# A second exchange through DRAM, read back by five transfers on one queue instead of four on two

## The chip, the cores and the metric

The kernel runs on one core of a Trainium2 chip. The metric is the device time of one execution in microseconds (us); lower is better. The kernel before takes 1402.76 us, the median of three runs (1402.32, 1402.76 and 1404.93).

The core's engines appear in the profile as PE (TensorE, the matrix engine, with PEld for its weight loads), DVE (VectorE), ACT (ScalarE), POOL (GpSimd) and SP (SyncE, which here only issues transfers). Each engine works off its own list of instructions in order and waits on semaphores for the others. A transfer is issued by an instruction on an engine's list and lands later; the profile lists the issuing instructions as SPq and ACTq.

## What is computed

Two layers of the same pair: a spectral filter over a 2048 x 512 activation, then multi-query attention with 32 heads of 16 columns that share one key and one value head.

```python
def _A_ref(x, w_r, w_i):
    X = rfft2(x.astype(float32))            # 2048 x 512 -> 2048 x 257
    X = X * (w_r + 1j * w_i)
    return irfft2(X, s=(S, D)).astype(bfloat16)

def _B_ref(x, wq, wk, wv, wo):
    q = (x @ wq) in 32 heads of 16; k = x @ wk; v = x @ wv
    p = softmax(q k^T * 16 ** -0.5)
    return (p v, heads joined) @ wo

x = x + _A_ref(layernorm(x)); x = x + _B_ref(layernorm(x))
x = x + _A_ref(layernorm(x)); x = x + _B_ref(layernorm(x))
```

## The kernel before

**The spectral layer.** `spectral_layer` does the 2-D transform as matrix products. A transform of length 2048 is split into 128 x 16, and between its two steps the data have to change their place across the 128 partitions. That is done by an exchange: tiles are written from the on-chip memory to a DRAM buffer and read back in another order. There are two exchanges in a layer, one on the way forward (D1) and one on the way back (D2). The columns stand in two halves, h = 0 and h = 1, and each half is exchanged by itself.

**The second exchange.** `back(j)` (lines 361 to 376) finishes a step of the inverse transform: PE computes, ACT (for the last piece DVE, line 373) copies the result into B1, and SP issues a write of 128 KB from B1 to D2 (line 376). Eight such writes make one half. `cross2` (lines 378 to 380) reads D2 back into B2. B2 holds 16 tiles t of 128 x 256 for each half; four reads of 256 KB bring tiles 0 to 3, 4 to 7, 8 to 11 and 12 to 15. All eight writes of a half must have landed before its first read is issued, since each read takes rows of every write. For h = 0 all four reads are issued by SP (line 392). For h = 1 they are issued by SP, ACT, SP and ACT in turn (line 421). In the profile both exchanges' buffers appear without their numbers: `D<-B` is a write of line 376, `B<-D` a read of line 379.

**What stands before and behind the reads of h = 1.** In program order: eight calls of `along(q, 0, ...)`, which multiply the 16 tiles of h = 0 (two tiles for each q; PE line 401) and copy the result into AT (ACT line 404, DVE line 406); then the reads of h = 1; in the first layer also the loads of two weights, wq and wo, on SP (`weights(20)`, lines 1225 and 1226); then `last(t, 0)` for t = 0 to 3 (PE lines 414 to 416), which need only h = 0. Then a loop over q = 0 to 8 (lines 427 to 443): `along(q, 1, True)` needs the tiles 2q and 2q + 1 of h = 1 and is copied by ACT; one round later `last` finishes the sums of the tiles 2q - 2 and 2q - 1, ACT copies them into x_sb (line 435), and DVE takes their mean and variance for the next layer norm (`norm.stats`, lines 157 and 158). Every fourth tile POOL and DVE complete the norm, and the attention's transposes, keys, values and first queries (lines 200 to 205, 472 to 526) are put between the later rounds.

**The order of the work.** The order on PE, ACT, DVE and SP is the order of the program text; nothing reorders it. The attention layer behind it orders its work by a planner's cost model at build time. Its long run of exponentials on ACT (line 1099) begins when the spectral layer ends.

Each read has a completion semaphore of its own, and PE's weight load of the first tile of a read waits for it.

```python
for q in range(8):
    along(q, 0, q % 2 == 0)
for g in range(4):
    cross2(1, g, (nc.sync, nc.scalar)[g % 2])
weights(20)
early = 4
for t in range(early):
    last(t, 0)
```

Of the kernel before, what the change touches and what calls it, by code (L numbers as in the profile page):

```python
# [218 lines left out]
def spectral_layer(nc, tc, tabs, ht, A_w_r, A_w_i, x_sb, bigp, pre, norm, att, feed, weights):  # L219
    C1, S1, S1N, PH, ident = (tabs[n] for n in ("C1", "S1", "S1N", "PH", "ident"))  # L220
    with tc.tile_pool(name="workA", bufs=2) as work, tc.tile_pool(name="tabA", bufs=1) as tabA, \
# [34 lines left out]
        D2 = dram.tile([2, P, 16, 256], BF, name="D2")  # L256
# [70 lines left out]
        Z, B1, B2 = big("Z"), big("B1"), big("B2")  # L327
        M = big("M").rearrange("p h t c -> p (h t c)").rearrange("p (i j b r f) -> p i j b r f", i=2, j=4, b=4, r=2)

        def filtered(j):  # L330

            h, b4 = j // 4, 4 * (j % 4)
            hf = slice(128 * h, 128 * h + 128)
            X = work.tile([P, 4, 2, 128], BF, name="X", tag="X", bufs=3)
            for b in range(b4, b4 + 4, 2):
                ps = bank()
                for i in range(2):
                    rotate(nc, ps[:, i, :], G[:, 0, :], G[:, 1, :], G[:, 2, :], A2[:, h, b + i, :], i == 0)
                nc.scalar.copy(out=X[:, b - b4:b - b4 + 2, :, :], in_=ps.rearrange("p j (r f) -> p j r f", r=2))
            m1, m2 = (M[:, i, j % 4] for i in range(2))  # L340
            wrb = wr_sb[:, b4:b4 + 4, hf].unsqueeze(2).to_broadcast([P, 4, 2, 128])
            wib = wi_sb[:, b4:b4 + 4, hf].unsqueeze(2).to_broadcast([P, 4, 2, 128])
            nc.vector.tensor_tensor(out=m1, in0=X, in1=wrb, op=ALU.mult)
            joined()
            nc.vector.tensor_tensor(out=m2, in0=X, in1=wib, op=ALU.mult)
            if j in DIRECT:
                unsummed[j] = (m1, m2)
            else:
                products.append((j, m1, m2))
# [3 lines left out]
        def joined():  # L353

            while products:
                j, m1, m2 = products.pop()
                Zv = Z[:, j // 4, 4 * (j % 4):4 * (j % 4) + 4, :].rearrange("p b (r f) -> p b r f", r=2)
                nc.vector.tensor_tensor(out=Zv[:, :, 0, :], in0=m1[:, :, 0, :], in1=m2[:, :, 1, :], op=ALU.subtract)
                nc.vector.tensor_tensor(out=Zv[:, :, 1, :], in0=m1[:, :, 1, :], in1=m2[:, :, 0, :], op=ALU.add)

        def back(j):
            h, b4 = j // 4, 4 * (j % 4)
            for b in range(b4, b4 + 4, 2):
                ps = bank()
                for i in range(2):
                    if j in DIRECT:
                        m1, m2 = (m[:, b + i - b4].rearrange("p r f -> p (r f)") for m in unsummed[j])
                        rotate(nc, ps[:, i, :], H1[:, b + i, :], H2N[:, b + i, :], H2[:, b + i, :], m1, i == 0, True, False)
                        rotate(nc, ps[:, i, :], H2N[:, b + i, :], H1N[j % 4][:, b + i - b4, :], H1[:, b + i, :], m2, False, False)
                    else:  # L370
                        rotate(nc, ps[:, i, :], H1[:, b + i, :], H2N[:, b + i, :], H2[:, b + i, :], Z[:, h, b + i, :], i == 0)
                if j == 7 and b > b4:
                    nc.vector.tensor_copy(out=B1[:, h, b:b + 2, :], in_=ps)
                else:
                    nc.scalar.copy(out=B1[:, h, b:b + 2, :], in_=ps)
                nc.sync.dma_start(out=D2[h, :, b:b + 2, :], in_=B1[:, h, b:b + 2, :])

        def cross2(h, g, eng):
            eng.dma_start(out=B2[:, h, 4 * g:4 * g + 4, :],
                          in_=D2[h].rearrange("(t a) b c -> t (a b) c", t=16)[4 * g:4 * g + 4].rearrange("t m c -> m t c"))  # L380

        for step in STEPS.split():
            j = int(step[1:] or 0)
            if step[0] == "f":
                filtered(j)
            elif step[0] == "b":
                back(j)
            elif step[0] == "j":
                joined()
            else:  # L390
                for g in range(4):
                    cross2(0, g, nc.sync)

        AT = big("AT").rearrange("p h t c -> p (h t c)").rearrange("p (t h c) -> p t h c", t=16, h=2)

        def along(q, h, use_scalar):

            ps = bank()
            for i in range(2):
                for j in range(2):  # L400
                    nc.tensor.matmul(ps[:, i, :], lhsT=B2[:, h, 2 * q + i, 128 * j:128 * j + 128], rhs=CS[:, j, :],
                                     start=(j == 0), stop=(j == 1), skip_group_check=True)
            if use_scalar:
                nc.scalar.copy(out=AT[:, 2 * q:2 * q + 2, h, :], in_=ps)
            else:
                nc.vector.tensor_copy(out=AT[:, 2 * q:2 * q + 2, h, :], in_=ps)
# [10 lines left out]

        for q in range(8):
            along(q, 0, q % 2 == 0)
        for g in range(4):  # L420
            cross2(1, g, (nc.sync, nc.scalar)[g % 2])
        weights(20)
        early = 4
        for t in range(early):
# [2 lines left out]
        for q in range(9):  # L427
# [9 lines left out]
            g, odd = divmod(q - 3, 2)  # L437
# [746 lines left out]
def full_kernel(ctx, tc, A_x, A_w_r, A_w_i, B_x, B_wq, B_wk, B_wv, B_wo, out):  # L1184
# [63 lines left out]
    for layer in range(2):  # L1248
        norm_in, norm_out = make_norm(), make_norm()
        spectral_layer(nc, tc, tabs, ht, A_w_r, A_w_i, x_sb, bigp, norm, norm_in, att, feed,  # L1250
                       weights if layer == 0 else lambda k: None)
        feed = attention_layer(nc, tc, att, norm_in, norm_out, x_sb, wo_sb, None if layer == 0 else store)
        norm = norm_out
# [47 lines left out]
```

## Time and profile before

| | us |
|---|---|
| median of three runs | 1402.76 |
| the profiled execution, its own time | 1402.49 |
| its span, first to last instruction | 1400.7 |
| PE busy in the span | 1348.2 (96%) |
| ACT busy | 1331.4 (95%) |
| DVE busy | 1305.8 (93%) |
| POOL busy | 849.4 (61%) |

What lies around the span is 1402.49 - 1400.7 = 1.8 us. The granted TensorE clock is 1.000 over the span. The first layer's second exchange falls at about 47 to 70 us, the second layer's at about 739 to 761 us; in the list of 40 equal slices of the span these are the slices in which PE, ACT and DVE are less busy than in the attention.

How to read it: the span is one line of waits and work, from the first instruction to the last. The chain of waits follows it back from the end; a piece of work that is not in the chain can be longer or shorter without moving the end, up to the point where it enters the chain. In the timeline a row has its start, its duration, engine, line and operation, and in brackets how long the engine stood idle before it and which event ended that. The list of transfers gives for each group of issues the size and the median time from issue to landing.

### The profile page before, as it was taken

How to read it: one execution, taken by the hardware profiler on the slowest of the kernel's cores; microseconds unless marked ns; L12 is line 12 of the kernel's file. 1: busy time of each engine (PE TensorE's matmuls, PEld its weight loads, DVE VectorE, ACT ScalarE, POOL GpSimd, SP SyncE). 2: the span in 40 equal slices, each digit the busy share in tenths (PEclk: the TensorE clock that was granted, in tenths of full speed). 3: DMA queues.
4: the chain of work that ended last, by engine and by line, in shares of the span. 5: the costliest groups of instructions: out<-in, count | busy, mean ns of one | idle time of the engine just before them, and what ended most of it. 6: DMA issues, size and time to landing. Idle time of an engine off the chain costs nothing.

```text
span 1400.7 us, 35023 instructions
## 1 busy us (share of the span) xinstructions
PE 1348.2 (96%) x14146; PEld 477.7 (34%) x14214; DVE 1305.8 (93%) x2253; ACT 1331.4 (95%) x1542; POOL 849.4 (61%) x507
## 2 busy tenths in 40 slices
PE   7899999999999999999999999999999999999998
PEld 6752232222222222222277422322223222222222
DVE  5689999999999999999966899999999999999997
ACT  6679999999999999999957899999999999999997
POOL 3325666667666667666640367666667667666664
PEclk9999999999999999999999999999999999999999
DMA  8700000000000000002064000000000000000000
GB/s 243 209 17 2 1 2 2 2 2 2 2 1 1 2 2 2 2 1 37 11 166 137 2 2 2 2 1 9 5 6 2 6 9 5 2 6 5 9 2 16
DMA packets 45395, 32.70 MB, mean 23 GB/s; under 512 B 10160, under 2 KB 43184, under 8 KB 44720
## 3 DMA queue, kind: packets, MB, share of 16 engines
q1 hardware_dynamic: 42832, 29.24, 7.4%
q8 instruction: 111, 1.82, 0.5%
q10 hardware_dynamic: 2400, 1.21, 0.3%
q14 instruction: 52, 0.43, 0.1%
HBM read 18.39 MB, written 10.49 MB: 21 GB/s over the span
## 4 chain that ended last, share of the span: by engine, by line
ACT 48%; PE 33%; issue 9%; DVE 6%; DMA 2%; POOL 1%; SPq 0%; DVEq 0%; ACTq 0%; POOLq 0%
ACT e L1099 47%; PE pv L888 13%; PE sc L933 10%; DVE ph L973 3%; PE aux L933 2%; PE ps L214 1%; PE ps L275 1%; DVE ln_stats L157 1%; PE aux L472 1%; DMA B<-D 1%; DVE ph L1005 1%; PE pv L903 1%; PE aux L701 1%; POOL tab_H L266 1%; PE ps L216 1%
## 5 line engine op out<-in xcount | busy, mean ns | idle before, releaser
L1099 ACT ACTIVATE e<-sc 128x1024 bf16<-128x1024 f32 x1328 | 1218.1, 1163 | 2.9 <-PE sc L933 2.9
L997 POOL TENSOR_TENSOR ph<-ph,step 128x1024 int32<-128x1024 int32 x404 | 763.3, 1893 | 412.3 <-DVE ph L1005 291.8
L973 DVE TENSOR_SCALAR ph<-aux 128x512 uint16<-128x512 f32 x1440 | 904.0, 679 | 20.4 <-PE aux L933 15.8
L888 PE MATMUL pv<-ph,vaug 128*32 128x512 bf16 x4320 | 548.8, 386 | 0.6 <-POOL ph L997 0.3
L933 PE MATMUL sc<-QT,Kv 32*128 32x512 bf16 x2656 | 521.9, 380 | 23.2 <-ACT e L1099 15.9
L888 PE MATMUL pv<-e,vaug 128*32 128x512 bf16 x2656 | 484.0, 384 | 0.3 <-ACT e L1099 0.3
L933 PE MATMUL aux<-QT,Kv 32*128 32x512 bf16 x1440 | 456.0, 384 | 1.0 <-DVE ph L973 0.5
L933 PEld LDWEIGHTS <-Kv 32*128 32x128 bf16 x4096 | 183.2, 91 | 525.5 <-issue 517.2
L903 PE MATMUL pv<-wo_sb,zeros 128*32 128x512 bf16 x1200 | 257.9, 383 | 0.0
L888 PEld LDWEIGHTS <-vaug 128*32 128x32 bf16 x6976 | 147.7, 94 | 293.0 <-issue 282.0
L1005 DVE TENSOR_SCALAR ph<-ph 128x2048 uint16<-128x2048 uint16 x316 | 216.6, 685 | 0.5
L163 POOL TENSOR_TENSOR ln_rstd<-ln_veps,mhalf 128x4 f32<-128x4 f32 x16 | 16.5, 1034 | 107.2 <-DVE ln_veps L162 107.1
L157 DVE BATCH_NORM_STATS2 ln_stats<-x_sb 128x6 f32<-128x512 bf16 x64 | 43.5, 679 | 23.3 <-ACT x_sb L435 17.2
L903 PEld LDWEIGHTS <-zeros 128*32 128x32 bf16 x1200 | 60.1, 94 | 1.9 <-issue 0.3
L803 DVE STREAM_TRANSPOSE oT<-pv 128x512 f32<-128x512 f32 x64 | 45.3, 707 | 9.2 <-PE pv L888 9.2
L186 ACT ACTIVATE Pk<-ps,ln_rstd 128x256 bf16<-128x256 f32 x64 | 26.7, 473 | 21.0 <-PE ps L275 16.1
L289 DVE CAST A<-ps 128x512 bf16<-128x512 f32 x28 | 19.2, 689 | 19.8 <-PE ps L216 18.7
L275 PE MATMUL ps<-tab_PH,xT 128*128 128x256 bf16 x256 | 35.6, 288 | 1.7 <-DMA tab_PH<-const_PH 0.8
L472 PE MATMUL aux<-xTa,wq_sb 128*128 128x512 bf16 x90 | 32.6, 385 | 2.8 <-issue 2.4
L825 POOL TENSOR_TENSOR on<-oT,rden 128x512 bf16<-128x512 f32 x30 | 31.7, 1058 | 2.0 <-DVE rden L829 1.8
L701 PE MATMUL aux<-wo_sb,ph 128*128 128x512 bf16 x72 | 26.1, 383 | 3.6 <-issue 2.1
L275 PEld LDWEIGHTS <-xT 128*128 128x128 bf16 x256 | 25.4, 103 | 6.0 <-issue 1.5
(117 smaller groups left out, 715.2 us busy)
## 6 DMA issues: line engine op xcount, KB each, us to landing
D<-A SPq DMA_DIRECT2D x32, 128.0 KB, 2.7
A<-D SPq DMA_DIRECT2D x16, 256.0 KB, 3.3
D<-B SPq DMA_DIRECT2D x32, 128.0 KB, 3.0
B<-D SPq DMA_DIRECT2D x12, 256.0 KB, 3.9
wr_sb<-in_A_w_r_dram SPq DMA_DIRECT2D x2, 1024.0 KB, 7.0
wi_sb<-in_A_w_i_dram SPq DMA_DIRECT2D x2, 1024.0 KB, 8.9
out_dram<-x_sb SPq DMA_DIRECT2D x15, 128.0 KB, 1.7
x_sb<-in_A_x_dram SPq DMA_DIRECT2D x3, 512.0 KB, 8.2
```

The source lines that it names most:

```text
L157: nc.vector.bn_stats(st, src)
L275: nc.tensor.matmul(ps[:, j, :], lhsT=xT[:, cc, 2 * k + j, :], rhs=PH[:, cc, 256 * h:256 * h + 256], start=(cc == 0), stop=(cc == NC - 1), ...
L472: self.nc.tensor.matmul(ps, lhsT=w(c), rhs=self.xTq[:, c, qc * 512:(qc + 1) * 512], start=(c == 0), stop=(c == NC - 1), skip_group_check=True)
L701: nc.tensor.matmul(ps, lhsT=OTs[qb][:, g4, kk * P:(kk + 1) * P], rhs=wo_sb[:, g4, :], start=first, stop=last, skip_group_check=True)
L803: end = clock.now(clock.FLIP, lambda: nc.vector.transpose(out=oT[:, par].rearrange("p b c -> p (b c)"), in_=pv), clock.last + clock.MM_END)
L888: nc.tensor.matmul(pv_tiles[gi][32 * i:32 * i + 32, :], lhsT=vaug[:, kc, j, :], rhs=es, start=((gi, i) not in started), stop=(left[gi, i] ...
L903: nc.tensor.matmul(pv_tiles[gi][32 * i:32 * i + 32, :], lhsT=att.zeros, rhs=wo_sb[:, 0, :], start=False, stop=False, skip_group_check=True)
L933: nc.tensor.matmul(out, lhsT=Kv[r, par, kc * P:(kc + 1) * P], rhs=QT[r, g, qb * 512:(qb + 1) * 512], start=True, stop=True, skip_group_che ...
L973: end = clock.now(clock.Z, lambda: nc.vector.tensor_scalar(out=z.bitcast(U16), in0=ps, scalar1=SCALE * LOG2E * 128.0, scalar2=127.0 * 128. ...
L997: nc.gpsimd.tensor_tensor(out=copy.bitcast(I32), in0=z.bitcast(I32), in1=step.to_broadcast([P, w // 2]), op=ALU.add)
L1005: nc.vector.tensor_scalar(out=one.bitcast(U16), in0=z.bitcast(U16), scalar1=float(PHASE[1]), scalar2=None, op0=ALU.add)
L1099: nc.scalar.activation(out=e[:, 0:ng * 512], in_=sc[:, 0:ng, :].rearrange("p a b -> p (a b)"), func=ACT.Exp, scale=SCALE)
```

## The change

For h = 1 all reads are issued by SP, and the first read of 256 KB is split into two of 128 KB (tiles 0 and 1, tiles 2 and 3). The three others keep their size. `cross2` now takes a first tile and a count. The calls for h = 0 read the same tiles on the same queue as before.

```diff
-        def cross2(h, g, eng):
-            eng.dma_start(out=B2[:, h, 4 * g:4 * g + 4, :],
-                          in_=D2[h].rearrange("(t a) b c -> t (a b) c", t=16)[4 * g:4 * g + 4].rearrange("t m c -> m t c"))
+        def cross2(h, t, n):
+            nc.sync.dma_start(out=B2[:, h, t:t + n, :],
+                              in_=D2[h].rearrange("(t a) b c -> t (a b) c", t=16)[t:t + n].rearrange("t m c -> m t c"))
...
-                    cross2(0, g, nc.sync)
+                    cross2(0, 4 * g, 4)
...
-        for g in range(4):
-            cross2(1, g, (nc.sync, nc.scalar)[g % 2])
+        for t, n in ((0, 2), (2, 2), (4, 4), (8, 4), (12, 4)):
+            cross2(1, t, n)
         weights(20)
```

In the built programs, SP issues five reads of h = 1 in place of two, in each layer; ACT issues none in place of two. PE, DVE, POOL and the rest of ACT have the same instructions in the same order. In the changed program PE's first product of h = 1 (q = 0) waits for the first read of 128 KB, the next (q = 1) for the second, and q = 2 for the read of tiles 4 to 7.

## The prediction, made before the changed kernel was run

> **What bounds the kernel now.** I read the span and the chain on the profile's page first, to see whether the place of the change lies on the path that sets the end.
>
> ```profile
> span 1400.7 us, 35023 instructions
> ...
> ACT 48%; PE 33%; issue 9%; DVE 6%; DMA 2%; POOL 1%; SPq 0%; DVEq 0%; ACTq 0%; POOLq 0%
> ```
>
> Transfers are 2% of the chain, some 28 us, and ACT's exponentials are most of it. A change to four reads in each layer can move only the part of those 2% that belongs to them. So next I took the chain in order of time around the end of each spectral layer (start, duration, what), first layer, then second:
>
> ```profile
> 63.76 3.35 DMA B<-D
> ...
> 67.16 0.62 PE ps L401 x4
> ```
>
> ```profile
> 755.76 3.32 DMA B<-D
> 759.08 0.05 issue
> 759.12 0.62 PE ps L401 x4
> ...
> 761.67 0.70 DVE ln_stats L157
> ...
> 788.26 6.10 ACT e L1099 x7
> ```
>
> The reader is to see that the first read of h = 1 is on the chain in both layers, with 3.35 and 3.32 us, and that PE starts 0.04 to 0.05 us after it has landed. Behind it the chain goes through PE, ACT and DVE into the attention, without another transfer; no row between lets the gain escape to something that starts by itself. So each microsecond by which this first read lands earlier moves everything behind it, until PE is held by something else. What that is, the timeline of PE shows:
>
> ```profile
> 65.34 0.38 PE L416 MATMUL ps<-tab_PSS,AT 128*128 128x512 bf16 x1
> 67.16 1.05 PE L401 MATMUL ps<-tab_CS,B 128*128 128x256 bf16 x8 [1.43 <-DMA B<-D]
> 69.32 0.60 PE L401 MATMUL ps<-tab_CS,B 128*128 128x256 bf16 x4
> ```
>
> ```profile
> 757.29 0.38 PE L416 MATMUL ps<-tab_PSS,AT 128*128 128x512 bf16 x1
> 759.12 1.05 PE L401 MATMUL ps<-tab_CS,B 128*128 128x256 bf16 x8 [1.46 <-DMA B<-D]
> 760.41 0.39 PE L415 MATMUL ps<-tab_PSC,AT 128*128 128x512 bf16 x1 [0.24 <-ACT AT L404]
> 761.28 0.60 PE L401 MATMUL ps<-tab_CS,B 128*128 128x256 bf16 x4
> ...
> 765.18 0.60 PE L401 MATMUL ps<-tab_CS,B 128*128 128x256 bf16 x4
> ```
>
> PE's sums of h = 0 end at 65.72 and 757.67, and then PE stands for 1.43 and 1.46 us. These two gaps are all that the change can win: 1.43 + 1.46 = **2.89 us**, 0.21% of the time. A forecast far outside that needs another mechanism, and I find none.
>
> **The change part by part.** Below, times with a plus are counted from the first read's issue (63.76 and 755.76).
>
> *The ACT queue is no longer used.* The issues in question:
>
> ```profile
> 63.76 0.92 SPq L379 DMA_DIRECT2D B<-D  x2
> 64.72 0.51 SPq L1225 DMA_DIRECT2D wq_sb<-in_B_wq_dram  x1
> ```
>
> ```profile
> 755.78 1.00 ACTq L379 DMA_DIRECT2D B<-D  x2
> 759.77 1.07 ACT L404 CAST AT<-ps 128x512 bf16<-128x512 f32 x2 [4.51 <-PE ps L401]
> ```
>
> ACT spends 1.00 us on its two issues, inside a gap of some 4.5 us in which it waits for PE. Taking them away is worth 0; were there no gap, it would be worth at most 1.00 us a layer. What counts is the company that the first read loses. In the first half (h = 0) the same read of 256 KB is issued by SP alone. Its issues, in the chain of the second layer (the fourth's piece runs on to its landing) and in the timeline of the first:
>
> ```profile
> 746.20 0.37 SPq L379
> ...
> 746.62 0.50 SPq L379
> ...
> 747.16 0.51 SPq L379
> ...
> 747.71 4.87 DMA B<-D
> ```
>
> ```profile
> 54.55 2.50 SPq L379 DMA_DIRECT2D B<-D  x4
> ```
>
> The list of transfers, for a window round the first issue alone, at 746.20 and at 54.55, gives the time to its landing:
>
> ```profile
> B<-D SPq DMA_DIRECT2D x1, 256.0 KB, 2.5
> ```
>
> ```profile
> B<-D SPq DMA_DIRECT2D x1, 256.0 KB, 2.7
> ```
>
> So without a read issued beside it the same 256 KB land at +2.5 and +2.7, not +3.32 and +3.35. The second queue's read, issued 0.02 us after the first, takes its share of the same engines: 0.82 us in the second layer, 0.65 in the first. [...]
>
> *The first read is halved.* How much sooner do 128 KB land than 256? No 128 KB read of this form is in the trace. The windows over the lone read of 746.20 show its bytes come in (last column, GB/s, in quarter microseconds):
>
> ```profile
> 747.25:747.50 0.25, 0.25 (x6) 0.19 (x3) 0.25 (x2) 0.25 (x2) 0.00 (x0) 1.00 0.71 207
> 747.50:747.75 0.25, 0.22 (x4) 0.09 (x2) 0.25 (x2) 0.25 (x1) 0.00 (x0) 1.00 0.92 281
> 747.75:748.00 0.25, 0.25 (x4) 0.23 (x5) 0.25 (x1) 0.25 (x2) 0.00 (x0) 1.00 1.08 330
> 748.00:748.25 0.25, 0.25 (x7) 0.23 (x4) 0.21 (x1) 0.25 (x1) 0.00 (x0) 1.00 1.23 330
> ```
>
> That is 52, 70, 82 and 82 kB: 128 KB (131 kB) are through at about 747.77, 256 KB at about 748.17. The second half of the bytes takes 0.40 us. So the first 128 KB should land at 2.5 - 0.4 = +2.1 in the second layer and 2.7 - 0.4 = +2.3 in the first. Bounds: not later than the whole read, +2.5 and +2.7; not sooner in effect than the end of PE's sums, +1.9 and +2.0. One more row lies near, in the chain: the last 128 KB write of a half, with nothing issued behind it.
>
> ```profile
> 744.05 2.00 DMA D<-B
> ```
>
> I take +2.1 and +2.3. [...]
>
> The gain of the first wait: second layer 3.32 - 2.1 = 1.22, first 3.35 - 2.3 = 1.05.
>
> *The second 128 KB* are issued about 0.42 us behind (746.62 - 746.20). As a lone whole read they would land at 0.42 + 2.5 = +2.9 and 0.42 + 2.7 = +3.1; as the second part of a 256 KB read at about +2.6 and +2.8. PE is through with q = 0 at 2.1 + 0.04 + 0.62 = +2.76 (+2.96 in the first layer), and then had 0.24 us to spare before line 415, which waits for ACT's copy of q = 0. So q = 1 may start at +3.0 (+3.2) at no cost, and even the late bounds fit. Cost 0.
>
> *The read of tiles 4 to 7* was issued on ACT at +0.02. It is now SP's third issue, at about +0.96 (747.16 - 746.20). Its landing before, from windows round ACT's first issue of the second and of the first layer:
>
> ```profile
> B<-D ACTq DMA_DIRECT2D x1, 256.0 KB, 3.7
> ```
>
> ```profile
> B<-D ACTq DMA_DIRECT2D x1, 256.0 KB, 3.8
> ```
>
> By then 512 KB were through, as they must be now. In the first half of the second layer the second read (issue 746.62) and the third (747.16) landed so long after their own issue:
>
> ```profile
> B<-D SPq DMA_DIRECT2D x1, 256.0 KB, 3.9
> ```
>
> ```profile
> B<-D SPq DMA_DIRECT2D x1, 256.0 KB, 4.6
> ```
>
> That is +4.3 for 512 KB and +5.56 for the third issue; those shared the engines with the writes of h = 1, which are over here. I take +4.0, with +3.7 and +5.56 as ends. PE needs it at q = 2: 761.28 - 755.76 = +5.52 and 69.32 - 63.76 = +5.56 before, so +4.30 and +4.51 once the gain is in. Behind it lies a little slack, from ACT's copy of tile 2 to DVE's turn for it:
>
> ```profile
> 762.49 0.62 ACT L435 CAST x_sb<-ps 128x512 bf16<-128x512 f32 x1
> ```
>
> ```profile
> 763.29 0.66 DVE L157 BATCH_NORM_STATS2 ln_stats<-x_sb 128x6 f32<-128x512 bf16 x1
> ```
>
> 763.29 - 763.11 = 0.18 us. At +4.0 the read costs nothing; from about +4.5 on it becomes the next wait.
>
> *The last two reads* are needed at q = 4 (765.18, +9.4) and q = 6, two rounds later. The fourth read of the first half, the latest of all, landed at +6.4. Cost 0.
>
> *The weights wq and wo* stand behind three more issues on SP, at some 0.55 us each (747.71 - 747.16), so 1.65 us later. wq took 6.1 us from its issue at 64.72; it would land by about 72.5, and PE first reads it here:
>
> ```profile
> 81.07 0.81 PE L472 MATMUL ps<-xTa,wq_sb 128*128 128x512 bf16 x3
> ```
>
> Eight us to spare. SP has nothing else in its list until the attention. Cost 0.
>
> **The sum:** 1.22 + 1.05 = 2.27 us less, 1402.49 - 2.27 = **1400.2 us**. The profiled execution is 0.27 us under the median of 1402.76; against that median it would be 1400.5.
>
> **The rivals.**
>
> *The whole gap closes.* If the first 128 KB land by +1.95, PE runs on from the sums of h = 0 and the gain is 2.89: 1399.6 us. For it: the write of the same size at 2.0. Against it: the lone reads of 2.5 and 2.7 less 0.4.
>
> *The split brings nothing,* because what is fixed in a transfer decides: landing as the lone whole reads, gain 0.82 + 0.65 = 1.47, 1401.0 us. For it: bytes begin to arrive only about 1 us after the issue, and the landing comes about 0.5 us after the last. Against: 0.40 us of the rest is bytes.
>
> *Tiles 4 to 7 become the wait.* If that third issue lands as the third one of the first half, at +5.56, q = 2 starts as late as before but for the slack: gain 5.52 + 0.18 - 5.56 = 0.14 and 5.56 + 0.18 - 5.56 = 0.18, together 0.32: 1402.2 us. Against it: the 512 KB that were through at +3.7.
>
> *Slower.* One queue hands out its reads so slowly that tiles 4 to 7 land like the fourth read of the first half, 747.71 + 4.87, which is +6.4; then q = 2 is 6.4 - 5.70 = 0.7 late in the second layer and 0.66 in the first, 1.4 us in all: 1403.9 us. It decides from a landing of +5.7 on. What speaks for it is that five issues follow one another on one sequencer. [...] Against it: the fourth read carried twice the bytes before it.
>
> **How the numbers follow.** Forecast 0.50, whole gap 0.13, no worth of the split 0.20, tiles 4 to 7 the wait 0.10, slower 0.07. The runs before spread from 1402.32 to 1404.93, so medians can differ by half a microsecond for nothing. The range takes the whole gap less that half (1399.1) and reaches up past the lost split and the third read to 1402.4; the slower rival is left out. For chances the bound is 0.2% of 1402.76, 2.8 us, about what a measurement of this kernel can tell from no change. Faster by more needs nearly the whole gap, or the forecast with scatter on its side: 0.32. Within: 0.60. Slower by over 2.8 us has no mechanism here that reaches it, only the slow rival with scatter: 0.08.
>
> **What would show it right or wrong.** In the chain, the two `DMA B<-D` pieces ahead of PE line 401 at 2.1 to 2.3 us; PE's idle time before line 401 at some 0.2 to 0.4 us; no wait for `B<-D` before q = 2. Were that idle time over 0.6, the split would be worth little; were there a new wait for `B<-D` before the third group of line 401, the third read is late. The forecast is wrong if the span shortens by less than 1.4 or more than 2.9 us, or if the two layers gain differently by more than 0.5.

## The result, and the profile after

The changed kernel takes 1401.38 us, the median of 20 runs (1399.77 to 1403.71); the kernel before, run beside it, 1403.86 us (20 runs, 1401.88 to 1406.72). The ratio is 0.9983 with a 95% interval of 0.9977 to 0.9989, so 1.5 to 3.2 us less. That is faster by less than the 0.2% that the prediction took for its bound, and inside its range of 1399.1 to 1402.4. The profiled execution took 1400.14 us with a span of 1398.3 us, 2.4 us less than before.

The chain of waits of the changed kernel, in order of time, around the second exchange of the first and of the second layer (start, duration, what):

```profile
63.49 2.10 DMA B<-D
...
65.64 0.62 PE ps L401 x4
...
68.19 0.71 DVE ln_stats L157
```

```profile
754.34 2.29 DMA B<-D
...
756.68 0.62 PE ps L401 x4
...
759.23 0.70 DVE ln_stats L157
```

The pieces are the same as before, in the same order. Only the first has shrunk: 3.35 to 2.10 us and 3.32 to 2.29 us. From there to DVE's first statistics it is 2.55 us in both kernels (68.19 - 65.64, 759.23 - 756.68, before 761.67 - 759.12).

The timeline of PE in the changed kernel, at the same two places:

```profile
64.57 0.38 PE L416 MATMUL ps<-tab_PSS,AT 128*128 128x512 bf16 x1
65.64 1.15 PE L401 MATMUL ps<-tab_CS,B 128*128 128x256 bf16 x8 [0.69 <-DMA B<-D]
...
67.80 0.60 PE L401 MATMUL ps<-tab_CS,B 128*128 128x256 bf16 x4
```

```profile
756.03 0.38 PE L416 MATMUL ps<-tab_PSS,AT 128*128 128x512 bf16 x1
756.68 1.05 PE L401 MATMUL ps<-tab_CS,B 128*128 128x256 bf16 x8 [0.27 <-DMA B<-D]
757.97 0.39 PE L415 MATMUL ps<-tab_PSC,AT 128*128 128x512 bf16 x1 [0.24 <-ACT AT L404]
...
758.85 0.60 PE L401 MATMUL ps<-tab_CS,B 128*128 128x256 bf16 x4
```

PE still waits for the first read, 0.69 and 0.27 us in place of 1.43 and 1.46. The eight products of q = 0 and q = 1 run through as one group; in the first layer they take 1.15 us for 1.05, since q = 1 had 0.1 us to wait for the second 128 KB. No wait for a read stands at q = 2. The read of tiles 4 to 7, in the list of transfers for a window round its issue, first and second layer:

```profile
B<-D SPq DMA_DIRECT2D x1, 256.0 KB, 3.1
```

```profile
B<-D SPq DMA_DIRECT2D x1, 256.0 KB, 3.4
```

Issued at +0.93, it landed at +4.05 and +4.29; q = 2 began at +4.31 and +4.51. It was in time by 0.2 to 0.3 us.

Where the 2.4 us of the span came from can be read off four marks: the first read's issue, and ACT's last copy into x_sb before the attention's exponentials. The timeline of ACT before (first and second layer), then after:

```profile
91.42 0.59 ACT L435 CAST x_sb<-ps 128x512 bf16<-128x512 f32 x1
...
783.39 0.59 ACT L435 CAST x_sb<-ps 128x512 bf16<-128x512 f32 x1
```

```profile
89.91 0.58 ACT L435 CAST x_sb<-ps 128x512 bf16<-128x512 f32 x1
...
780.96 0.58 ACT L435 CAST x_sb<-ps 128x512 bf16<-128x512 f32 x1
```

| stretch | before | after | difference |
|---|---|---|---|
| start to the first read of h = 1, first layer | 63.76 | 63.49 | -0.27 |
| that read to the last copy | 27.66 | 26.42 | **-1.24** |
| to the first read of h = 1, second layer | 664.34 | 664.43 | +0.09 |
| that read to the last copy | 27.63 | 26.62 | **-1.01** |
| to the end of the span | 617.31 | 617.34 | +0.03 |

The two stretches that hold the changed reads give 2.25 us, the rest 0.15. The attention is the same length to a tenth of a microsecond.

### The profile page after: what moved, and what is told of

It reads as the page before. It is cut to its first block, busy times and chain, and to the rows that moved or that the text cites. A ratio compares the mean times of both kernels' runs of the same rounds, so it can differ in the third digit from the quotient of the medians.

```text
span 1398.3 us, 35025 instructions
## 1 busy us (share of the span) xinstructions
PE 1347.1 (96%) x14146; PEld 476.9 (34%) x14214; DVE 1306.7 (93%) x2253; ACT 1331.1 (95%) x1542; POOL 849.7 (61%) x507
## 4 chain that ended last, share of the span: by engine, by line
ACT 49%; PE 32%; issue 9%; DVE 7%; DMA 2%; POOL 1%; SPq 0%; DVEq 0%; ACTq 0%; POOLq 0%
ACT e L1099 48%; PE pv L888 12%; PE sc L933 10%; DVE ph L973 3%; PE aux L933 2%; PE ps L214 1%; PE ps L275 1%; DVE ln_stats L157 1%; PE aux L472 1%; DVE ph L1005 1%; DMA B<-D 1%; PE ps L216 1%; PE pv L903 1%; PE aux L701 1%; PE ps L215 1%
```

## The experiments

Twelve runs, in three series; each ratio is to the kernel before, run in the same series. A landing with a plus is counted from the first read's issue. "Read to exponential" is the time from that issue to the moment when ACT's list comes to the first exponential of the attention: before 28.15 and 28.11 us, changed kernel 26.89 and 27.09 us (first and second layer). In every trace the exponential itself starts 1.32 us later, when PE's first scores are there; the differences are the same for both.

**The changed kernel again (c1), no edit.**

> The changed kernel once more, as the yardstick on this chip and for a second trace of the two first reads. Theory (less company and half the bytes): first 128 KB at +2.1 to +2.3 after their issue in each layer, PE's first product of h = 1 at +2.15 to +2.35 (before: +3.40 and +3.36), ratio to the kernel before 0.998. Rival (the 2.4 us are scatter of the attention or of the first half, not the reads): the reads land so again, but the time differs by less than 1 us from before.

Measured: 1401.71 us, ratio 0.9981 (0.9971 to 0.9990). First 128 KB at +2.00 and +2.14, read to exponential 27.18 and 26.93: 2.15 us less than before. In the first layer three reads in a row were late for PE:

```profile
66.42 0.61 PE L401 MATMUL ps<-tab_CS,B 128*128 128x256 bf16 x4 [0.27 <-DMA B<-D]
67.33 0.61 PE L401 MATMUL ps<-tab_CS,B 128*128 128x256 bf16 x4 [0.29 <-DMA B<-D]
68.97 0.61 PE L401 MATMUL ps<-tab_CS,B 128*128 128x256 bf16 x4 [0.16 <-DMA B<-D]
```

The rows are q = 0, 1 and 2. The second 128 KB came at +2.90 and tiles 4 to 7 at +4.54; the stretch behind q = 0 was 0.39 us longer for it (25.14 for 24.75). So the theory holds, and the rival of the prediction in which tiles 4 to 7 become the wait is real in some executions, at a few tenths.

**One queue without the split (e1, run twice).**

```diff
-        for t, n in ((0, 2), (2, 2), (4, 4), (8, 4), (12, 4)):
+        for t, n in ((0, 4), (4, 4), (8, 4), (12, 4)):
```

> All reads of h = 1 on SP, none split: 4 x 256 KB. Theory: the first read lands at +2.5 to +2.75, as the lone reads of h = 0 do; 0.65 to 0.82 us of the first wait go in each layer, 1.5 us in all against the kernel before, so some 0.8 us slower than the changed kernel (ratio to before about 0.9989). Rival A (the split brings nothing, the one queue all): first read at +2.1 to +2.3, time as the changed kernel. Rival B (the split brings all): first read still at +3.3, time as before.

> One queue, no split, a second time. Its first trace showed 0.50 and 0.55 us less from the first read's issue to the first exponential, but its runs showed no gain (ratio 0.9999, interval 0.9988 to 1.0010). Theory (the local gain reaches the end): ratio near 0.9993 over both batches. Rival (the company on the other queue costs nothing at the end): 1.0000 again, and the trace's first read at +3.3.

Measured: first 1404.80 us, ratio 0.9999 (0.9988 to 1.0010), then 1403.45 us, ratio 0.9990 (0.9979 to 1.0000). The first reads in the chains, first and second layer of the first run, then of the second:

```profile
65.15 2.85 DMA B<-D
...
757.24 2.78 DMA B<-D
```

```profile
65.56 2.91 DMA B<-D
...
758.11 2.75 DMA B<-D
```

Four landings at +2.75 to +2.91, mean 2.82, where the theory said +2.5 to +2.75. Both rivals fall: the queue alone is worth 3.34 - 2.82 = 0.52 us a layer, neither all nor nothing (3.34 is the mean of the two landings in the one trace of the kernel before). The first run's ratio, no gain, would have misled if taken alone. The local gain, 1.05 us in two layers in the first trace, is a ratio of 0.9993, which lies in both intervals; but so does 1.0000, and the runs alone show no gain. The clock does not set the two runs apart: both traces have PE at half clock for 3.4 us ahead of the first layer's reads, from 46.66 and from 46.32 us on.

**Split, but with company (e2).**

```diff
-        def cross2(h, t, n):
-            nc.sync.dma_start(out=B2[:, h, t:t + n, :],
+        def cross2(h, t, n, eng=nc.sync):
+            eng.dma_start(out=B2[:, h, t:t + n, :],
...
-        for t, n in ((0, 2), (2, 2), (4, 4), (8, 4), (12, 4)):
-            cross2(1, t, n)
+        for t, n, eng in ((0, 2, nc.sync), (4, 4, nc.scalar), (2, 2, nc.sync), (8, 4, nc.sync), (12, 4, nc.scalar)):
+            cross2(1, t, n, eng)
```

> The first read split, but two whole reads stay on ACT: SP issues tiles 0-1, 2-3 and 8-11, ACT issues 4-7 and 12-15. Theory: the company takes its share; in the trace of before 256 KB of both queues together were through 0.4 to 0.5 us later than the lone 256 KB's first half, so tiles 0-1 land at +2.6 to +2.8 and tiles 2-3 at +3.2 to +3.4; PE's first product at about +2.7, and q = 1 waits a further 0.1 to 0.3 us. Gain against before 0.4 to 0.7 us a layer, 0.8 to 1.4 us in all. Rival (only the size of the first read counts): +2.1 to +2.3 and the time of the changed kernel.

Measured: 1404.48 us, ratio 1.0000 (0.9989 to 1.0011). Tiles 0 and 1 at +2.57 and +2.27, tiles 2 and 3 at +3.89 and +4.38. PE in the second layer:

```profile
759.45 0.61 PE L401 MATMUL ps<-tab_CS,B 128*128 128x256 bf16 x4 [1.39 <-DMA B<-D]
761.55 1.04 PE L401 MATMUL ps<-tab_CS,B 128*128 128x256 bf16 x4 [1.49 <-DMA B<-D]
```

The first piece comes early all the same, but then the next piece of the same queue goes beside ACT's 256 KB (the engines moved 301 to 310 GB/s for both queues together from 759 to 761 us), and the wait reappears at q = 1 with 1.49 us. The four products of q = 1 also take 1.04 us for 0.61: PE ran at a clock of 0.50 there, of which more below. The theory put the two landings at +2.6 to +2.8 and +3.2 to +3.4 and the gain at 0.8 to 1.4 us; the first came sooner than that and the second later. Read to exponential is 27.83 and 29.70 us, 0.3 less than before in the first layer and 1.6 more in the second, and the runs show no gain. Here the split pays nothing while another 256 KB go beside its other half.

**The two halves on two queues (e4).**

```diff
-        for t, n in ((0, 2), (2, 2), (4, 4), (8, 4), (12, 4)):
-            cross2(1, t, n)
+        for t, n, eng in ((0, 2, nc.sync), (2, 2, nc.scalar), (4, 4, nc.sync), (8, 4, nc.sync), (12, 4, nc.sync)):
+            cross2(1, t, n, eng)
```

> Tiles 0-1 on SP and tiles 2-3 on ACT at the same time, all the rest on SP. Theory: 256 KB go together, so tiles 0-1 land between a lone 128 KB and a lone 256 KB, +2.3 to +2.7, tiles 2-3 about +0.1 later; PE's first product 0.2 to 0.4 us later than in the changed kernel, in each layer: 0.4 to 0.8 us slower than it. Rival (a second queue takes nothing, it saves the issue time of SP): tiles 0-1 at +2.1 to +2.3, tiles 2-3 0.4 us sooner than in the changed kernel, time the same or 0.1 us better.

Measured: 1401.77 us, ratio 0.9980 (0.9971 to 0.9989). Tiles 0 and 1 at +2.43 and +2.25, tiles 2 and 3 at +2.81 and +2.63, read to exponential 27.36 and 27.05: 1.85 us less than before, 0.43 us more than the changed kernel. The chain of the second layer:

```profile
755.20 2.25 DMA B<-D
...
757.50 0.62 PE ps L401 x4
```

Tiles 0 and 1 land a little behind a lone half (mean 2.14), as the theory says; tiles 2 and 3 come 0.38 us behind them and not 0.1, but q = 1 did not wait. The loss against the changed kernel is within the expected 0.4 to 0.8 us; the runs can't tell a difference of 0.4 us.

**Tiles 4 to 7 read last (e3).**

```diff
-        for t, n in ((0, 2), (2, 2), (4, 4), (8, 4), (12, 4)):
+        for t, n in ((0, 2), (2, 2), (8, 4), (12, 4), (4, 4)):
```

> The changed kernel's five reads on SP, with the read of tiles 4 to 7 issued last instead of third. It measures how much room that read has. In the traces of the changed kernel the fifth read lands at +5.9 to +7.0, and PE reaches q = 2 at +4.3 to +4.5. Theory (it has 0.2 us of room behind q = 2 and becomes the wait after that): q = 2 starts at +5.9 to +6.9, 1.3 to 2.3 us later per layer than in the changed kernel, so 2.6 to 4.6 us slower than it and not faster than the kernel before. Rival (rounds q = 2 and later have slack in the chain of DVE): less than 0.5 us a layer.

Measured: 1404.52 us, ratio 1.0006 (0.9997 to 1.0015), some 3 us over the changed kernel in the other series. PE in the second layer, q = 0, 1 and 2:

```profile
759.03 0.61 PE L401 MATMUL ps<-tab_CS,B 128*128 128x256 bf16 x4 [0.48 <-DMA B<-D]
759.79 0.61 PE L401 MATMUL ps<-tab_CS,B 128*128 128x256 bf16 x4 [0.15 <-DMA B<-D]
762.87 0.61 PE L401 MATMUL ps<-tab_CS,B 128*128 128x256 bf16 x4 [1.51 <-DMA B<-D]
```

The fifth read landed at +6.06 and +5.86. q = 2 began 4.02 and 3.84 us behind q = 0 in place of 2.16, that is 1.86 and 1.68 us late, and from q = 0 to the first exponential it took 26.61 and 26.44 us for 24.75: 1.86 and 1.69 more. The whole lateness comes through. There is no room behind q = 2, not even the 0.2 us that the prediction and this expectation read from DVE's turn.

**Three products to fill PE's gap (e5).** They write a bank that nothing reads.

```diff
         for t in range(early):
             last(t, 0)
+        fill = psum.tile([P, 512], F32, name="ps", tag="pa")
+        for _ in range(3):
+            nc.tensor.matmul(fill, lhsT=ident, rhs=PSC[:, 0, :], start=True, stop=True, skip_group_check=True)
```

> The changed kernel with three more products on PE (0.22 us each, written to a bank that nobody reads) behind the early sums of h = 0, where PE waits for the first read. Of the eleven runs and traces of the changed kernel that came with lower mean clock, the trace of another kernel shows why: PE at half clock for 3.4 us behind a gap. Theory F (the gaps ahead of q = 0 are what drops the clock): more runs at clock 1.000 than the changed kernel's 11 of 30, the median 0.5 to 1 us lower, ratio to before about 0.9975. Rival G (the drops come from other places): same share of runs at 1.000, time the same or up to 0.4 us slower where the fill delays q = 0.

Measured: 1401.95 us, ratio 0.9988 (0.9979 to 0.9997); 5 of 11 runs at a clock of 1.000. Read to exponential 27.15 and 26.92; in the first layer the fill held q = 0 back to +2.42 though the read was there at +2.02. No gain, and the share of runs at full clock says nothing either way: inconclusive. Its trace holds a stretch of half clock from 47.28 to 50.69 us, ahead of the reads, so not every drop comes from the gap that the products fill.

**Five early sums (e6, run twice).**

```diff
-        early = 4
+        early = 5
```

> The changed kernel with the early sums of h = 0 done for five tiles instead of four: three products of 0.22 us move from behind q = 3 into the gap ahead of q = 0. If PE's later rounds are covered by DVE's chain, the moved work was worth nothing and the time stays, or is 0 to 0.5 us worse a layer where the sums end later than the first read lands (they ended at +1.3 to +2.1, so at +1.95 to +2.7 then). If PE sets those rounds, 0.65 us a layer are won. I expect no gain in the chain, and the effect on the clock of the kernel with three added products.

> Five early sums instead of four, a second time. First trace: 26.78 and 26.85 us from the first read's issue to the first exponential, 0.1 to 0.35 us a layer better than the changed kernel's traces; runs 0.9978 to before. Theory (the sums fill a gap and take a little off PE's later rounds): 0.2 to 0.6 us better than the changed kernel beside it. Rival (scatter): equal within 0.3 us.

Measured: 1400.99 us, ratio 0.9978 (0.9969 to 0.9987), and 1401.62 us, ratio 0.9974 (0.9964 to 0.9985); the changed kernel beside the second, 1402.06 us. Read to exponential 26.78 and 26.85 in the first trace, 27.05 and 26.77 in the second. PE in the second layer of the first:

```profile
757.66 1.07 PE L401 MATMUL ps<-tab_CS,B 128*128 128x256 bf16 x8 [0.35 <-DMA B<-D]
758.95 0.39 PE L415 MATMUL ps<-tab_PSC,AT 128*128 128x512 bf16 x1 [0.22 <-ACT AT L404]
```

Where no read was late, q = 0 to the first exponential took 24.62 to 24.68 us for 24.75: of 0.65 us moved, 0.1 is won. The two traces, 53.63 and 53.82 us for both layers together, lie just under the changed kernel's 53.88 to 54.11, and the runs don't separate the two.

**All 16 tiles in one read (e7).**

```diff
-        for t, n in ((0, 2), (2, 2), (4, 4), (8, 4), (12, 4)):
+        for t, n in ((0, 16),):
```

> All 16 tiles of h = 1 in a single read of 1 MB on SP. Theory: the bytes decide; 1 MB at about 300 GB/s is through 3.3 us after its first byte, the read lands at +5.3 to +6.3, PE's first product then, 3.1 to 4.1 us later than in the changed kernel in each layer, and PE's gap of 3.5 to 4.5 us is followed by a stretch of half clock of 3.4 us that costs another 1 to 1.7 us where PE sets the pace. Time 6 to 11 us over the changed kernel. Rival (a gap alone does not drop the clock): 6 to 8 us, granted clock 1.000 behind the gap.

Measured: 1413.02 us, ratio 1.0064 (1.0052 to 1.0077), some 11 us over the changed kernel in the other series, the upper end of what was expected. The read landed at +6.45 and +6.17 (expected +5.3 to +6.3). PE in the first layer, and the windows there (the columns behind POOL are the granted clock, the share of the DMA engines and GB/s):

```profile
71.24 1.89 PE L401 MATMUL ps<-tab_CS,B 128*128 128x256 bf16 x8 [5.31 <-DMA B<-D]
```

```profile
71.00:74.00 3.00, 2.76 (x11) 1.47 (x12) 0.00 (x0) 1.17 (x2) 0.00 (x0) 0.50 0.72 230
```

A gap of 5.31 us, then the clock at 0.50, and eight products in 1.89 us for 1.05. The rival falls.

**Six reads and five early sums (e8).**

```diff
-        for t, n in ((0, 2), (2, 2), (4, 4), (8, 4), (12, 4)):
+        for t, n in ((0, 2), (2, 2), (4, 2), (6, 2), (8, 4), (12, 4)):
...
-        early = 4
+        early = 5
```

> Five early sums, and the read of tiles 4 to 7 split into two of 128 KB as well: six reads on SP. In the traces of the changed kernel that read landed at +3.9 to +4.5, PE wanted it at +4.3 to +4.6, and in one of four it held q = 2 back by about 0.2 us. Theory: tiles 4-5 land at +3.3 to +4.0 and q = 2 never waits; 0 to 0.2 us a layer better than five early sums alone. Rival (each further issue of about 0.5 us pushes the later tiles out and the wait moves to q = 3): tiles 6-7 at +4.6 or later, q = 3 waits, 0 to 0.4 us worse.

Measured: 1401.70 us, ratio 0.9971 (0.9960 to 0.9983), against 0.9974 for five early sums alone in the same series. Tiles 4 and 5 landed at +3.63 and +3.29, tiles 6 and 7 at +4.69 and +4.05; neither q = 2 nor q = 3 waited for its read:

```profile
69.41 0.61 PE L401 MATMUL ps<-tab_CS,B 128*128 128x256 bf16 x4 [0.51 <-DMA B<-D]
70.35 0.61 PE L401 MATMUL ps<-tab_CS,B 128*128 128x256 bf16 x4 [0.33 <-DMA B<-D]
71.66 0.60 PE L401 MATMUL ps<-tab_CS,B 128*128 128x256 bf16 x4
```

Here, in the first layer, q = 1 waited for its 128 KB (+3.05), which the extra reads don't help; in the second layer the fifth sum held q = 0 back to +2.42 though its read was there at +2.19. No difference to five early sums alone can be told.

**The changed kernel a third time (c2), no edit.**

> The changed kernel a third time, beside the three below on one chip. Its traces so far: from the first read's issue to the first exponential 26.89 to 27.18 us in a layer (before: 28.15 and 28.11), 2.15 to 2.28 us less in all. Theory: again 2.0 to 2.4 us less, ratio 0.998. If the time of the runs followed something else, the ratio would leave 0.9975 to 0.999.

Measured: 1402.06 us, ratio 0.9978 (0.9968 to 0.9987); first 128 KB at +2.15 in both layers, read to exponential 26.94 twice: 2.38 us less than before.

## Why the prediction was right

**What bounds.** The first read of h = 1 was on the chain and still is, and what it gives up reaches the end undiminished: 2.25 us in the two stretches, 2.4 us in the span. c1 and c2 repeat it with 2.15 and 2.38.

**The sum.** Predicted 1.05 + 1.22 = 2.27 us; in the changed kernel's first trace, 1.26 + 1.02 = 2.28 from the read to the exponential. Measured against its own time, 1402.49, the profiled execution came out at 1400.14 for 1400.2. The medians are higher, in both kernels: the kernel before ran 1403.86 in 20 runs where three had given 1402.76.

**The terms.** The mechanism was right, but that the sum came so close is luck: it was better than its terms, whose errors cancel. Taking the company away was put at 0.82 and 0.65 us; e1 shows 0.52 on the mean of four. Halving the read was put at 0.40 us; the six first reads of the changed kernel land at +2.00 to +2.29, mean 2.14, so it is worth 2.82 - 2.14 = 0.68. These are the worths in this order, queue first. With a second queue at work, e2 has the half at +2.42 on the mean of two against 3.34 for the whole, so there the halving is worth 0.92 and the queue then 0.28. The cause of the first error is in the trace: the price of a lone whole read came from two samples, 2.5 and 2.7. In the fourteen traces there are 28 such reads of h = 0; they land at 2.53 to 2.97, half of them at 2.78 or later, and 2.53 is the lowest of all. It made the queue look better and, by the subtraction, the split worse. Once the whole read is put at 2.8, 0.40 us off give +2.4, which is 0.26 too late: that part of the gain is more than the bytes between the first and the second 128 KB. Where it comes from was not tried and stays open. The layers were not different either: +2.3 and +2.1 were forecast for the first and the second, and they came as +2.10 and +2.29. So the gains by layer, 1.05 and 1.22 in the forecast, came the other way round, 1.26 and 1.02.

**The rest of SP's list.** No trace shows ACT's two issues as a cost or a gain, as predicted. The second 128 KB came at +2.65 and +2.69 (forecast +2.6 to +2.8) and cost 0.1 us in one layer. Tiles 4 to 7 came at +4.05 and +4.29 (forecast +4.0). Here the prediction's margin was too kind: the 0.18 us of slack that it read from DVE's turn is not there, as e3 shows. DVE's turn left that room, but PE's list behind q = 2 moves as a whole, and the exponentials wait for the end of that list: in the chain of the kernel before, first layer, PE's rows run from 79.58 us to the first scores at 92.74 with no gap over 0.1 us. The read was in time by 0.22 to 0.26 us, no more, and in c1 it wasn't.

**The rivals.** "The split brings nothing" is refuted by e1 against the changed kernel, "the whole gap closes" by PE's waits of 0.69 and 0.27. The cap of 2.89 us rested on PE's early sums ending at +1.9 to +2.0; they ended at +1.46 and +2.07 here, and at +0.9 to +2.0 in the other traces whose PE list up to there is the same. So a larger gap can be left than one trace of before shows, and the cap was no cap. For the same reason one of the prediction's signs misled: an idle time of PE over 0.6 us was to mean that the split is worth little. It was 0.69 in the first layer, where the read landed at +2.10 and the gain was the larger one; PE had only ended its early sums sooner. The slower rival, a landing behind +5.7, is what e3 builds: +5.9 to +6.1, and the kernel is not faster than before.

## What to carry to other kernels

When an engine stands waiting for the first piece of a larger transfer, give that piece a transfer of its own, just large enough for the first step, and let nothing run beside it: here the absence of a second queue was worth 0.52 us and, on the one queue, the smaller size 0.68. The pieces behind it must follow in the order in which they are used, since a late one takes the place of the wait that was removed (in e3, q = 2 was 1.86 and 1.68 us late). Take the price of a transfer from as many samples as the trace has; two of them hid a spread of 0.4 us.

## What was not expected

**PE's clock stood at half behind stretches with little work.** The windows of e2's second layer: the stretch at half clock, and as long a stretch ahead of it and behind:

```profile
757.55:760.97 3.42, 1.11 (x7) 0.32 (x5) 0.00 (x0) 0.58 (x1) 0.00 (x0) 1.00 0.76 222
760.97:764.38 3.41, 2.83 (x10) 1.43 (x11) 0.29 (x1) 1.22 (x3) 0.00 (x0) 0.50 0.33 85
764.38:767.80 3.42, 3.42 (x21) 1.92 (x20) 3.13 (x9) 3.09 (x6) 0.00 (x0) 1.00 0.00 0
```

In 3.42 us PE was busy for 1.11; the next 3.41 us ran at half clock, then it was full again. The same in the first run of e1, at 43 to 50 us, where 0.90 us of work went ahead, and in the second, with 1.32 us:

```profile
43.25:46.66 3.41, 0.90 (x13) 0.72 (x12) 3.41 (x6) 0.98 (x3) 1.35 (x1) 1.00 0.69 189
46.66:50.08 3.42, 3.42 (x28) 2.89 (x26) 1.72 (x4) 1.70 (x3) 0.91 (x6) 0.50 0.88 249
```

```profile
42.90:46.32 3.42, 1.32 (x18) 1.09 (x16) 3.42 (x5) 1.80 (x4) 2.47 (x2) 1.00 0.56 158
46.32:49.73 3.41, 3.00 (x22) 2.59 (x23) 2.83 (x6) 1.17 (x2) 0.00 (x0) 0.50 0.93 261
```

PE was not idle ahead of these three drops, it was busy for 26 to 39% of the stretch. In the kernel before, two windows round the gap ahead of q = 0 held more work, 1.94 and 1.74 us of 3.40, and the clock stayed at 1.00:

```profile
756.00:759.40 3.40, 1.94 (x11) 0.84 (x10) 0.00 (x0) 0.00 (x0) 0.00 (x0) 1.00 0.72 213
757.70:761.10 3.40, 1.74 (x12) 1.03 (x13) 0.00 (x0) 1.12 (x3) 0.00 (x0) 1.00 0.92 250
```

How much work keeps the clock full was not tried.

**The runs' clocks.** Each run is listed with its mean granted clock. In the three series, the kernel before had 0.998 or less in 44 of 93 runs. The changed kernel had that in 1 of 22 runs in the two series with c1 and c2, and in 4 of its 20 runs in the result. A shorter gap ahead of q = 0 would fit that, and it would add to the gain of the medians (2.5 to 3.1 us) over that of the traces (2.15 to 2.38). It is not shown: no trace of the kernel before holds such a drop, the drops in the traces of both runs of e1 and of e5 come ahead of the reads, and e5, which filled the gap, told nothing.
